# A cached-attention decode block with its gradients on one core: another order of the forward loop with three V loads ahead in place of five, zero-padded dO copies filled once by VectorE, and four copies of transposed V moved to VectorE

## Chip, cores and metric

The kernel runs on one core of one Trainium2 chip. The metric is device time in microseconds (us), the median of several executions.

## What is computed

The reference is one pre-layernorm decode block (batch 4, one new token, width 512) and the gradients of all its inputs but one:

```python
def _A_ref(x, k_cache, v_cache, wq, wo):          # B=4, H=32 heads, Dh=128, Sk=4096 cached rows
    q = (x @ wq).reshape(B, Sq, H, Dh).transpose(0, 2, 1, 3)
    scores = einsum("bhqd,bhkd->bhqk", q, k_cache) * (Dh ** -0.5)
    p = softmax(scores)
    o = einsum("bhqk,bhkd->bhqd", p, v_cache)
    return o.transpose(0, 2, 1, 3).reshape(B, Sq, H * Dh) @ wo
...
h  = x + _A_ref(layernorm(x), k_cache, v_cache, wq, wo)
h2 = h + (silu(layernorm(h) @ w1) * (layernorm(h) @ w3)) @ w2
out, vjp = jax.vjp(f, x, k_cache, v_cache, wq, wo, w1, w3, w2);  grads = vjp(grad_out)
```

There are 4 x 32 = 128 pairs of batch and head, called heads here. Each has a K and a V of 4096 x 128 bf16, which is 1 MB each. The forward part reads all K and V once (268 MB). The backward part reads all V again (134 MB) and writes the gradients of K and V (268 MB).

## The kernel before

The order of the instructions is written out by hand: every engine runs its instructions in the order of the program, and waits only where data or a buffer is not ready.

**Slots.** On-chip memory has 23 slots of about 1 MB (`NSLOT`, class `Slot`, L108). A list `free` hands out the slot that was given back longest ago, in the order of the program. A transfer into a slot waits on SP's queue until the slot's last user is done, and all later transfers wait behind it. Loads of K (`load_K`, L139, issued at L142) and of V (`load_V`, L146, issued at L150) take one slot each; so do a head's transposed K (`KT`), its product P*K (`PK`, with a column pair holding P), and every group of 16 results `M` (eight such slots by the end of the forward part). `more_K(s)` (L153) loads K ahead until head s + 6, as long as more than one slot is free; V is loaded `VQ` = 5 heads ahead.

**Forward loop** (L625, 64 groups `gi` of two heads, a = 2 gi and a + 1). For a group:

- `S_head` (L339) makes the scores of the group's heads on TensorE from the transposed K; it gives the KT slots back.
- `T_pe` (L316) and `T_dve` (L325) transpose the K of the next group's two heads, na and nb: a quarter on TensorE with a copy on ScalarE (L322, L323), three quarters on VectorE (L328).
- The softmax: `sm_max` (VectorE, L361 mx, L363 mxm), `sm_max_T` (TensorE, x_ps L368), `sm_gmax` (VectorE, gm L373), `sm_bcast` (TensorE, b_ps L378), `sm_exp` (VectorE nm L383, ScalarE E L386), `sm_sum` (TensorE, l_ps L392), `sm_norm` (VectorE rl L397, ScalarE Pn L400), `sm_P` (TensorE pt_P L407, ScalarE P_all L411).
- `PK_pairs` (GpSimd, L417) takes a PK slot and writes P pairs into it; `PK_mul` (VectorE, L421) multiplies K by P and gives the K slot back.
- `M_mm` (TensorE, L436) multiplies PK by V; `M_end` adds sums for dq (L446), copies the result (ScalarE, L452) and gives the PK and V slots back.

Before, group gi multiplies P*K for head a - 2 between mxm and gm, and for head a - 1 at its end; `M_mm` runs for heads a - 3 and a - 2. Every 32 heads, `kP_copy` and, later in the group, `kP_columns` move a sum out. After the loop a tail finishes heads 125 to 127 and multiplies by wo; in the last groups `weights` (L595) loads wo, w1 and w3 as slots come free.

**Middle.** One chain of small operations: layernorm, w1 and w3 products (gu_ps L848), their gradients, dO for the first 32 of the 128 heads (`dO_columns`, L743), first gradients of V (`grad_V`, L788, VectorE L781, written out from L792). V is loaded for the second time at L808 into whatever slots are free.

**Backward loop.** `front(s)` (L1177) transposes V of head s in four groups (`V_T`, L768: TensorE L775, ScalarE copy L776) and multiplies it with dO, using four zero-padded copies `zd` of a dO column (L1193). The copies are zeroed and filled by GpSimd (L1154, L1158). `more_V` makes gradients of V, `grad_K` those of K (VectorE L781), and each 1 MB result is written out on SP's queue.

Of the kernel before, what the change touches and what calls it, by code (L numbers as in the profile page):

```python
# [10 lines left out]
BF16 = mybir.dt.bfloat16  # L11
# [2 lines left out]
AX = mybir.AxisListType  # L14

G = 2
VQ = 5
SLOT = 4160
NSLOT = 23
JQ = 8  # L20
# [4 lines left out]
def kernel(  # L25
# [22 lines left out]
    nc = tc.nc  # L48
    P = nc.NUM_PARTITIONS
# [101 lines left out]


    def more_K(s):  # L153
        while len(Ks) + kdone["n"] < min(NH, s + 7) and len(free) > 1:
            load_K(len(Ks) + kdone["n"])

    kdone = {"n": 0}
# [133 lines left out]
    def M_of(s):  # L291
        return Ms[s // MC].f(MC * (Dh + 1)).rearrange("p (n c) -> p n c", c=Dh + 1)[:, s % MC, :]
# [77 lines left out]
    def sm_gmax(gi):  # L370
        st = hold[gi]
        st["gm"] = fw.tile([G, 1], FP32, tag="gm", name="gm")
        nc.vector.tensor_reduce(out=st["gm"][:], in_=st["x"][0:G, 0:P], axis=AX.X, op=ALU.max)  # L373
# [45 lines left out]
    def PK_mul(s):  # L419
        PK = PKs[s].t[:].rearrange("p (j c) -> p j c", c=PKW)  # L420
        nc.vector.tensor_tensor(  # L421
            out=PK[:, :, 0:Dh].rearrange("p j (r t) -> p j r t", t=2),
            in0=Ks[s].heads().rearrange("p j (r t) -> p j r t", t=2),
            in1=PK[:, :, None, Dh:PKW].to_broadcast([P, SJ, Dh // 2, 2]),
            op=ALU.mult,
        )
        Ks.pop(s).give()
        kdone["n"] += 1
# [9 lines left out]
    def M_end(s):  # L438
        w = s % 32
        PK = PKs[s].t[:].rearrange("p (j c) -> p j c", c=PKW)  # L440
        if w == 0:
            hold["kP"] = psK.tile([P, 4, Dh], FP32, name="kP_ps", tag="kP")
        for c in range(2):
            for q in range(4):
                j0 = (c * 4 + q) * 4
                nc.tensor.matmul(hold["kP"][32 * q:32 * (q + 1), :, :], lhsT=ones_window(w), rhs=PK[:, j0:j0 + 4, 0:Dh],  # L446
                                 start=(w == 0 and c == 0), stop=(w == 31 and c == 1), tile_position=(0, 32 * q))
        PKs.pop(s).give()
        Vs.pop(s).give()
        if s % MC == 0:  # L450
            Ms.append(Slot("M"))
        nc.scalar.copy(out=M_of(s), in_=hold["M"][:, 0:Dh + 1])  # L452

    def kP_copy():
        hold["ks"] = Slot("kP_sb")
        kP_sb = hold["ks"].f(4 * Dh).rearrange("p (c d) -> p c d", c=4)
        nc.scalar.copy(out=kP_sb, in_=hold["kP"][:])

    def kP_columns(s):
        ks = hold.pop("ks")  # L460
        kP_sb = ks.f(4 * Dh).rearrange("p (c d) -> p c d", c=4)
        kt_ps = psM.tile([P, PKW], FP32, tag="M", name="kt_ps")
        for c in range(4):
            nc.tensor.matmul(kt_ps[:, 0:H], lhsT=kP_sb[:, c, :], rhs=sel_f[:], start=(c == 0), stop=(c == 3))
        nc.scalar.copy(out=kPT[:, s - 31:s + 1], in_=kt_ps[:, 0:H])
        ks.give()

    def O_cols(s0, s1):
        nc.vector.tensor_copy(out=OT_f[:, s0:s1], in_=Ms[s0 // MC].f(MC * (Dh + 1)).rearrange("p (n c) -> p n c", c=Dh + 1)[
            :, s0 % MC:s0 % MC + s1 - s0, Dh])  # L470
        nc.vector.tensor_copy(out=OT_bf[:, s0:s1], in_=OT_f[:, s0:s1])
# [123 lines left out]
    def weights(gi):  # L595
        if gi in reserve:
            while nvl["n"] < NH and len(free) > reserve[gi]:
                load_V(nvl["n"])
            pump(reserve[gi])
# [14 lines left out]

    def O_cols_of(m):
        if m % MC == MC - 1 and m < NH - 1:
            O_cols(m - MC + 1, m + 1)

    def PK(s):
        PK_mul(s)
        more_K(s + 1)

    for gi in range(NGI):  # L625
        nxt = gi < NGI - 1
        a, na, nb = gi * G, gi * G + 2, gi * G + 3
        m1, m2 = a - 3, a - 2
        has1, has2 = m1 >= 0, m2 >= 0
        S_head(gi, 0)  # L630
        S_head(gi, 1)
        weights(gi)
        if nxt:
            q_stationaries(gi + 1)
            T_pe(na)
        sm_max(gi)
        if has2:
            PK(m2)
        if has1:
            M_mm(m1, 0, 16)  # L640
        if nxt:
            T_pe(nb)
        sm_max_T(gi)
        sm_gmax(gi)
        if nxt:
            T_dve(na, 1)
        if has1:
            M_mm(m1, 16, SJ)
            M_end(m1)
            load_V(m1 + VQ)  # L650
            if m1 % 32 == 31:
                kP_copy()
        sm_bcast(gi)
        weights(gi)
        sm_exp(gi)
        if nxt:
            T_dve(na, 2)
            T_dve(na, 3)
        if has2:
            PK_pairs(a - 1)  # L660
            M_mm(m2, 0, 16)
        sm_sum(gi)
        sm_norm(gi)
        if gi == NGI - 1:

            nc.scalar.sqrt(warm[:], warm[:])
        if has1:
            O_cols_of(m1)
        if nxt:
            T_dve(nb, 1)  # L670
            T_dve(nb, 2, 2)
        if has2:
            M_mm(m2, 16, SJ)
            M_end(m2)
            load_V(m2 + VQ)
            PK(a - 1)
        weights(gi)
        if has1 and m1 % 32 == 31:
            kP_columns(m1)
        sm_P(gi)  # L680
        PK_pairs(a)
        weights(gi)
        hold.pop(gi - 3, None)
        if 2 <= gi:
            step("d")

    PK(NH - 2)
    c1b.close()
    c1b = ExitStack()
    psT = c1b.enter_context(tc.tile_pool(name="psTm", bufs=4, space=bass.MemoryType.PSUM))  # L690
# [21 lines left out]
    O_cols(NH - MC, NH)  # L712
    attn_page(2)
    attn_page(3)
    kP_copy()
    kP_columns(NH - 1)
    weights(NGI)
    assert not pending
    c1b.close()
# [16 lines left out]
    dqT_bf = pers2.tile([P, NH], BF16, name="dqT_bf")  # L736
    dqr_bf = pers2.tile([NH, Dh], BF16, name="dqr_bf")

    dhT = pers2.tile([P, DC, B], BF16, name="dhT")
    dhT_f = pers2.tile([P, DC, B], FP32, name="dhT_f")  # L740


    def dO_columns(h0, h1, ps, tag):  # L743
        s0, s1 = h0 * B, h1 * B
        dOT_ps = ps.tile([P, 512], FP32, tag=tag, name="dOT_ps")
        for h in range(h0, h1):
            for jj in range(DC):
                nc.tensor.matmul(dOT_ps[:, h * B:(h + 1) * B], lhsT=wo_page(h)[:, h % 8, jj, :], rhs=dhT[:, jj, :],
                                 start=(jj == 0), stop=(jj == DC - 1))
        nc.vector.tensor_copy(out=dOT_bf[:, s0:s1], in_=dOT_ps[:, s0:s1])  # L750
        nc.vector.tensor_tensor(out=dOT_f[:, s0:s1], in0=dOT_bf[:, s0:s1], in1=OT_f[:, s0:s1], op=ALU.mult)

    def dO_rows(h0, h1, ps_, tag_):
# [14 lines left out]
    def V_T(s, ps, part=range(SJ // GW)):  # L768
        if s not in VTs:
            VTs[s] = V2s.pop(s)  # L770
        v = VTs[s].heads()
        for g in part:
            pt = ps.tile([P, GW, P], BF16, tag="tps", name="pt_tps")
            for i in range(GW):
                nc.tensor.transpose(pt[:, i, :], v[:, g * GW + i, :], ident_b[:])  # L775
            nc.scalar.copy(out=v[:, g * GW:(g + 1) * GW, :], in_=pt[:])  # L776

    P2s, first_gv = {}, []

# [158 lines left out]
    with ExitStack() as c2:  # L938
# [210 lines left out]

        rows = {}  # L1150
        dS2s = {}
        zd = [bw3.tile([P, 132], BF16, name=f"zd{i}", tag=f"zd{i}", bufs=1) for i in range(B)]
        for i in range(B):
            nc.gpsimd.memset(zd[i][:], 0.0)  # L1154

        def dO_window(s):
            if s < NH:
                nc.gpsimd.tensor_copy(out=zd[s % B][:, 32:132:67], in_=dOT_bf[:, s:s + 1].to_broadcast([P, 2]))  # L1158

        def P_pairs(s):  # L1160
            if s < NH and s not in P2s:
# [15 lines left out]
        def front(s):  # L1177
            hl = s % B
            if s not in VTs:
                for g in range(SJ // GW):  # L1180
                    V_T(s, psT, range(g, g + 1))
                    if hl == 0 and g == 0:
                        rows_out()
                    if hl == 0 and g == 2:
                        rows_T()
            VT = VTs[s].heads()
            if hl == 0:
                rows["acc"] = psD.tile([P, 512], FP32, tag="dP", name="dP_ps")
            dO_window(s + 2)
            for u in range(2):  # L1190
                for c in range(4):
                    j0 = 8 * c + 4 * u
                    nc.tensor.matmul(rows["acc"][32 * c:32 * (c + 1), :], lhsT=zq_window(zd[hl], 2 * hl + u),  # L1193
                                     rhs=VT[:, j0:j0 + 4, :], start=(hl == 0 and u == 0),
                                     stop=(hl == B - 1 and u == 1), tile_position=(0, 32 * c))
            if hl == B - 1:
                rows["ps"] = rows.pop("acc")
            sl = VTs.pop(s)
            (vring if len(V2s) + len(VTs) + len(vring) < NV2 else free).append(sl.i)
# [46 lines left out]
            if s < NH and s not in V2s and s not in VTs:  # L1246
                load_V2(nc.sync)

        for s in range(2):
            dO_window(s)  # L1250
        for s in range(3, 6):
            P_pairs(s)
        for s in range(L):
# [60 lines left out]
```

## Time and profile before

| | us |
|---|---|
| median of 3 runs | 1728.51 |
| lowest and highest run | 1726.37, 1729.18 |
| the profiled execution's own time | 1729.18 |
| span of that execution's profile | 1727.3 |
| busy: TensorE matmul, VectorE, ScalarE, GpSimd | 1266.5, 1222.4, 974.2, 495.6 |
| bytes moved by DMA | 707.51 MB, mean 410 GB/s |

The profile's page divides the span in 40 slices of 43 us. The forward loop's first scores start at 19.8 us; the scores of group 57 start at 595.36, those of the last group, 63, at 678.60 us. The first gradient of V starts on its way out at 726.72 us. The last compute instruction ends at 1691 us, and what follows is the end of the writes. In views by stretch, the last three columns are the granted TensorE clock, the busy share of the DMA engines and GB/s. "L322 <- DMA Kn" in a view of waits means that the engine stood at line 322 until a load of K had landed.

### The profile page before, as it was taken

The page shows a single profiled execution, that of the slowest core. Times are in us where ns is not written, and L with a number is a line of the kernel's source. Part 1 is how long each engine was busy: PE and PEld are TensorE (multiplying, and loading weights), DVE is VectorE, ACT ScalarE, POOL GpSimd, SP SyncE. Part 2 cuts the span into 40 slices and gives each one's busy share as a digit, 9 for nine tenths or more (in the row PEclk, how much of TensorE's full clock was granted, in tenths as well). Part 3 has the DMA queues.
Part 4 walks back from the last instruction along what each step waited for, and adds up shares of the span by engine and source line. Part 5 has one row for each costly group of instructions (what it writes and reads, how often), then busy time and mean ns, then how long its engine had stood idle before and what let it go on. Part 6 is the DMA issues. An engine that isn't in the chain of part 4 may idle for free.

```text
span 1727.3 us, 38444 instructions
## 1 busy us (share of the span) xinstructions
PE 1266.5 (73%) x16180; PEld 916.7 (53%) x16180; DVE 1222.4 (71%) x1294; ACT 974.2 (56%) x1502; POOL 495.6 (29%) x678
## 2 busy tenths in 40 slices
PE   5899888888888877877777664666767567676550
PEld 4677666666666655745555443544444334443330
DVE  5899889898899866577776655674557556665672
ACT  3465545454454433577766664776767566576540
POOL 1344444444443322143243120131102222220020
PEclk9999999999999988799988997986888777788785
DMA  9999999999999978899999999999999999999996
GB/s 402 425 424 424 423 423 425 424 419 417 421 419 407 424 311 296 358 404 425 425 425 426 425 425 426 425 425 426 423 421 421 418 419 415 420 417 418 416 418 279
DMA packets 101742, 707.51 MB, mean 410 GB/s; under 512 B 11052, under 2 KB 15288, under 8 KB 17600
## 3 DMA queue, kind: packets, MB, share of 16 engines
q1 hardware_dynamic: 101152, 704.95, 98.1%
q8 instruction: 127, 2.08, 0.5%
q14 instruction: 47, 0.39, 0.1%
q0 software_dynamic: 416, 0.10, 0.0%
HBM read 422.59 MB, written 282.34 MB: 408 GB/s over the span
## 4 chain that ended last, share of the span: by engine, by line
DMA 50%; ACT 2%; PE 1%; DVE 1%; issue 0%; DVEq 0%; SPq 0%; ACTq 0%; POOL 0%
DMA out_dram<-gv 20%; DMA out_dram<-gk 14%; DMA V<-in_A_v_cache_dram 13%; ACT V L776 1%; DMA out_dram<-gwo 1%; DMA out_dram<-gw 1%; DMA wq<-in_A_wq_dram 1%; PE pt_tps L775 1%; DVE gv L781 1%; DVE gk L781 1%; PE dP_ps L1193 0%; PE gps L957 0%; ACT dPr L1168 0%; DVEq L1309 0%; PE rep_ps L1144 0%
## 5 line engine op out<-in xcount | busy, mean ns | idle before, releaser
L776 ACT COPY V<-pt_tps 128x1024 bf16<-128x1024 bf16 x512 | 489.9, 1024 | 134.2 <-PE pt_tps L775 126.3
L775 PE MATMUL pt_tps<-ident_b,V 128*128 128x128 bf16 x4096 | 350.2, 245 | 195.0 <-ACT V L776 154.4
L775 PEld LDWEIGHTS <-V 128*128 128x128 bf16 x4096 | 299.5, 112 | 267.0 <-issue 201.7
L781 DVE TENSOR_TENSOR gv<-P,reps 128x4096 bf16<-128x4096 bf16 x125 | 286.3, 2293 | 194.3 <-DMA out_dram<-gv 96.0
L781 DVE TENSOR_TENSOR gk<-dS,reps 128x4096 bf16<-128x4096 bf16 x128 | 293.2, 2293 | 104.4 <-DMA out_dram<-gv 88.9
L436 PE MATMUL M_ps<-PK,Vn 128*128 128x130 bf16 x4096 | 287.7, 223 | 9.2 <-DVE PK L421 7.1
L421 DVE TENSOR_TENSOR PK<-Kn,PK 128x4096 bf16<-128x4096 bf16 x128 | 290.0, 2265 | 2.3 <-POOL PK L417 2.1
L436 PEld LDWEIGHTS <-Vn 128*128 128x128 bf16 x4096 | 259.1, 100 | 18.2 <-issue 10.9
L328 DVE STREAM_TRANSPOSE KT<-Kn 128x512 f32<-128x512 f32 (+1 forms) x321 | 244.0, 791 | 0.2 <-issue 0.2
L323 ACT COPY KT<-pt_tps 128x1024 bf16<-128x1024 bf16 x128 | 129.4, 1012 | 194.2 <-PE pt_tps L322 163.2
L1193 PE MATMUL dP_ps<-V,zd 128*32 128x512 bf16 x1024 | 179.6, 430 | 68.8 <-ACT V L776 66.1
L1163 POOL COPY P<-P_all 128x64 bf16<-128x64 bf16 x125 | 94.6, 758 | 446.1 <-DVE gv L781 446.0
L417 POOL COPY PK<-P_all 128x64 bf16<-128x64 bf16 x128 | 74.0, 578 | 402.2 <-ACT P_all L411 267.7
L1158 POOL COPY zd<-dOT_bf 128x2 bf16<-128x2 bf16 x128 | 126.5, 989 | 168.8 <-PE dP_ps L1193 168.6
L334 POOL TENSOR_TENSOR W<-qrep,wmask 128x128 bf16<-128x128 bf16 x128 | 153.3, 1197 | 19.7 <-DVE qrep L286 14.5
L322 PE MATMUL pt_tps<-ident_b,Kn 128*128 128x128 bf16 x1024 | 83.5, 228 | 80.0 <-DMA Kn<-in_A_k_cache_dram 79.8
L1193 PEld LDWEIGHTS <-zd 128*32 128x32 bf16 x1024 | 37.4, 95 | 156.6 <-issue 141.9
L322 PEld LDWEIGHTS <-Kn 128*128 128x128 bf16 x1024 | 61.4, 102 | 108.3 <-DMA Kn<-in_A_k_cache_dram 104.0
L400 ACT ACTIVATE Pn<-E,rl 128x1024 bf16<-128x1024 f32 x64 | 73.7, 1151 | 49.5 <-DVE rl L397 44.4
L446 PE MATMUL kP_ps<-PK,onesw 128*32 128x512 bf16 x1024 | 81.1, 394 | 0.0
L354 PE MATMUL S_ps<-KT,W 128*32 128x256 bf16 x1536 | 75.0, 286 | 0.5 <-DVE KT L328 0.2
L411 ACT COPY P_all<-pt_P 32x64 bf16<-32x64 bf16 x256 | 52.1, 204 | 38.0 <-PE pt_P L407 35.7
(239 smaller groups left out, 1206.8 us busy)
## 6 DMA issues: line engine op xcount, KB each, us to landing
Kn<-in_A_k_cache_dram SPq DMA_DIRECT2D x128, 1024.0 KB, 14.1
Vn<-in_A_v_cache_dram SPq DMA_DIRECT2D x128, 1024.0 KB, 13.4
V<-in_A_v_cache_dram SPq DMA_DIRECT2D x128, 1024.0 KB, 20.0
out_dram<-gv SPq DMA_DIRECT2D x128, 1024.0 KB, 20.0
out_dram<-gk SPq DMA_DIRECT2D x128, 1024.0 KB, 20.1
wq<-in_A_wq_dram SPq DMA_DIRECT2D x8, 1024.0 KB, 15.4
out_dram<-gw SPq DMA_DIRECT2D x6, 896.0 KB, 19.9
wo<-in_A_wo_dram SPq DMA_DIRECT2D x4, 1024.0 KB, 8.1
```

The lines of the kernel that those rows point to most:

```text
L322: nc.tensor.transpose(pt[:, i, :], Kn[:, c * GW + i, :], ident_b[:])
L323: nc.scalar.copy(out=KT[:, c * GW:(c + 1) * GW, :], in_=pt[:])
L328: nc.vector.transpose(out=KT[:, c * w_:(c + n) * w_], in_=Kn[:, c * w_:(c + n) * w_])
L334: nc.gpsimd.tensor_tensor(out=W[:, hl], in0=qrep[:, :, s:s + 1].to_broadcast([P, 4, 32]), in1=wmask[:, hl, None, :].to_broadcast([P, 4, 32 ...
L421: nc.vector.tensor_tensor(out=PK[:, :, 0:Dh].rearrange("p j (r t) -> p j r t", t=2), in0=Ks[s].heads().rearrange("p j (r t) -> p j r t", t=2),
L436: nc.tensor.matmul(hold["M"][:], lhsT=Vn[:, j, :], rhs=PK[:, j, :], start=(j == 0), stop=(j == SJ - 1))
L775: nc.tensor.transpose(pt[:, i, :], v[:, g * GW + i, :], ident_b[:])
L776: nc.scalar.copy(out=v[:, g * GW:(g + 1) * GW, :], in_=pt[:])
L781: nc.vector.tensor_tensor(out=dst.rearrange("p j (r t) -> p j r t", t=2), in0=col2[:, :, None, :].to_broadcast([P, SJ, Dh // 2, 2]), in1=r ...
L1158: nc.gpsimd.tensor_copy(out=zd[s % B][:, 32:132:67], in_=dOT_bf[:, s:s + 1].to_broadcast([P, 2]))
L1163: nc.gpsimd.tensor_copy(out=P2s[s][:], in_=P_all[:, s, :, None].to_broadcast([P, SJ, 2]))
L1193: nc.tensor.matmul(rows["acc"][32 * c:32 * (c + 1), :], lhsT=zq_window(zd[hl], 2 * hl + u), rhs=VT[:, j0:j0 + 4, :], start=(hl == 0 and u ...
```

## The change

In the forward loop the order within a group is another one: `M_mm` for head a - 3 now comes right behind the scores; `T_dve(na, 1)`, not a P*K product, stands between mxm and gm; both P*K products of a group, for heads a - 1 and a, stand in its second half, the second as its last VectorE instruction. `VQ` is 3 in place of 5, and K is loaded up to one head further (`s + 8`). `kP_copy` and `kP_columns` become one `kP_flush` right behind `M_end`. In the middle, `zd` is one tile that GpSimd zeroes early, and one VectorE instruction fills it for the first four heads; for heads 1 to 4, VectorE copies the second of the four groups of transposed V.

```diff
-VQ = 5
+VQ = 3
...
-        while len(Ks) + kdone["n"] < min(NH, s + 7) and len(free) > 1:
+        while len(Ks) + kdone["n"] < min(NH, s + 8) and len(free) > 1:
...
     for gi in range(NGI):
...
         S_head(gi, 1)
         weights(gi)
+        if has1:
+            M_mm(m1, 0, 16)
+        sm_max(gi)
         if nxt:
             q_stationaries(gi + 1)
             T_pe(na)
-        sm_max(gi)
-        if has2:
-            PK(m2)
-        if has1:
-            M_mm(m1, 0, 16)
-        if nxt:
-            T_pe(nb)
+            T_dve(na, 1)
         sm_max_T(gi)
-        sm_gmax(gi)
-        if nxt:
-            T_dve(na, 1)
         if has1:
             M_mm(m1, 16, SJ)
+        sm_gmax(gi)
+        sm_bcast(gi)
+        if nxt:
+            T_dve(na, 2)
+        sm_exp(gi)
+        if has1:
             M_end(m1)
             load_V(m1 + VQ)
...
-        sm_bcast(gi)
-        weights(gi)
-        sm_exp(gi)
+        if hasp:
+            PK_pairs(pk1)
         if nxt:
-            T_dve(na, 2)
             T_dve(na, 3)
-        if has2:
-            PK_pairs(a - 1)
-            M_mm(m2, 0, 16)
+            T_pe(nb)
+            T_dve(nb, 1)
         sm_sum(gi)
         sm_norm(gi)
...
-        if nxt:
-            T_dve(nb, 1)
-            T_dve(nb, 2, 2)
+        if hasp:
+            PK_mul(pk1)
+            more_K(pk1 + 1)
+        weights(gi)
         if has2:
-            M_mm(m2, 16, SJ)
+            M_mm(m2, 0, 24)
+        sm_P(gi)
+        if has2:
+            M_mm(m2, 24, SJ)
             M_end(m2)
             load_V(m2 + VQ)
-            PK(a - 1)
         weights(gi)
-        sm_P(gi)
         PK_pairs(a)
+        if nxt:
+            T_dve(nb, 2, 2)
+        PK_mul(a)
+        more_K(a + 1)
         weights(gi)
...
+    zd = pers2.tile([P, B, 132], BF16, name="zd")
+    nc.gpsimd.memset(zd[:], 0.0)
...
         nc.vector.tensor_copy(out=dOT_bf[:, s0:s1], in_=dOT_ps[:, s0:s1])
+        if s0 == 0:
+            nc.vector.tensor_copy(out=zd[:, :, 32:132:67], in_=dOT_bf[:, 0:B, None].to_broadcast([P, B, 2]))
...
-            nc.scalar.copy(out=v[:, g * GW:(g + 1) * GW, :], in_=pt[:])
+            if 0 < s < 5 and g == 1:
+                nc.vector.tensor_copy(out=v[:, g * GW:(g + 1) * GW, :], in_=pt[:])
+            else:
+                nc.scalar.copy(out=v[:, g * GW:(g + 1) * GW, :], in_=pt[:])
...
-        zd = [bw3.tile([P, 132], BF16, name=f"zd{i}", tag=f"zd{i}", bufs=1) for i in range(B)]
-        for i in range(B):
-            nc.gpsimd.memset(zd[i][:], 0.0)
...
-            if s < NH:
-                nc.gpsimd.tensor_copy(out=zd[s % B][:, 32:132:67], in_=dOT_bf[:, s:s + 1].to_broadcast([P, 2]))
+            if B <= s < NH:
+                nc.gpsimd.tensor_copy(out=zd[:, s % B, 32:132:67], in_=dOT_bf[:, s:s + 1].to_broadcast([P, 2]))
...
-        for s in range(2):
-            dO_window(s)
```

In the diff, `m1` is a - 3, `m2` is a - 2 and `pk1` is a - 1; `has1`, `has2`, `hasp` and `nxt` only guard the first and last groups.

More of the change, by code (lines that the diff above doesn't have):

```diff
@@ L447, in M_end @@
                                  start=(w == 0 and c == 0), stop=(w == 31 and c == 1), tile_position=(0, 32 * q))
-        PKs.pop(s).give()
-        Vs.pop(s).give()
         if s % MC == 0:
@@ L452, in M_end, with kP_flush @@
         nc.scalar.copy(out=M_of(s), in_=hold["M"][:, 0:Dh + 1])
-    def kP_copy():
-        hold["ks"] = Slot("kP_sb")
-        kP_sb = hold["ks"].f(4 * Dh).rearrange("p (c d) -> p c d", c=4)
+        PKs.pop(s).give()
+        Vs.pop(s).give()
+    def kP_flush(s):
+        ks = Slot("kP_sb")
+        kP_sb = ks.f(4 * Dh).rearrange("p (c d) -> p c d", c=4)
         nc.scalar.copy(out=kP_sb, in_=hold["kP"][:])
-    def kP_columns(s):
-        ks = hold.pop("ks")
-        kP_sb = ks.f(4 * Dh).rearrange("p (c d) -> p c d", c=4)
         kt_ps = psM.tile([P, PKW], FP32, tag="M", name="kt_ps")
@@ L613 @@
             T_dve(s, c)
[L617 to L623, printed above, removed]
     for gi in range(NGI):
@@ L628 @@
         m1, m2 = a - 3, a - 2
-        has1, has2 = m1 >= 0, m2 >= 0
+        pk1 = a - 1
+        has1, has2, hasp = 0 <= m1 < NH, 0 <= m2 < NH, 0 <= pk1 < NH
         S_head(gi, 0)
@@ L651 @@
             if m1 % 32 == 31:
-                kP_copy()
-        sm_bcast(gi)
-        weights(gi)
-        sm_exp(gi)
+                kP_flush(m1)
+            if m1 % MC == MC - 1 and m1 < NH - 1:
+                O_cols(m1 - MC + 1, m1 + 1)
+        if hasp:
+            PK_pairs(pk1)
         if nxt:
-            T_dve(na, 2)
             T_dve(na, 3)
-        if has2:
-            PK_pairs(a - 1)
-            M_mm(m2, 0, 16)
+            T_pe(nb)
+            T_dve(nb, 1)
         sm_sum(gi)
@@ L666 @@
             nc.scalar.sqrt(warm[:], warm[:])
-        if has1:
-            O_cols_of(m1)
-        if nxt:
-            T_dve(nb, 1)
-            T_dve(nb, 2, 2)
+        if hasp:
+            PK_mul(pk1)
+            more_K(pk1 + 1)
+        weights(gi)
         if has2:
-            M_mm(m2, 16, SJ)
+            M_mm(m2, 0, 24)
+        sm_P(gi)
+        if has2:
+            M_mm(m2, 24, SJ)
             M_end(m2)
             load_V(m2 + VQ)
-            PK(a - 1)
         weights(gi)
-        if has1 and m1 % 32 == 31:
-            kP_columns(m1)
-        sm_P(gi)
         PK_pairs(a)
+        if nxt:
+            T_dve(nb, 2, 2)
+        PK_mul(a)
+        more_K(a + 1)
         weights(gi)
@@ L685 @@
             step("d")
-    PK(NH - 2)
     c1b.close()
@@ L714 @@
     attn_page(3)
-    kP_copy()
-    kP_columns(NH - 1)
+    kP_flush(NH - 1)
     weights(NGI)
@@ L1192, in front @@
                     j0 = 8 * c + 4 * u
-                    nc.tensor.matmul(rows["acc"][32 * c:32 * (c + 1), :], lhsT=zq_window(zd[hl], 2 * hl + u),
+                    nc.tensor.matmul(rows["acc"][32 * c:32 * (c + 1), :], lhsT=zq_window(zd[:, hl], 2 * hl + u),
                                      rhs=VT[:, j0:j0 + 4, :], start=(hl == 0 and u == 0),
```

## The prediction

> **What bounds the kernel now.** I read the page's slices first, then waits by stretch, then the DMA by ten-us stretches, then SP's own timeline.
>
> ```profile
> DMA  9999999999999978899999999999999999999996
> GB/s 402 425 424 424 423 423 425 424 419 417 421 419 407 424 311 296 358 404 425 425 425 426 425 425 426 425 425 426 423 421 421 418 419 415 420 417 418 416 418 279
> ```
>
> The DMA is full nearly everywhere, at some 424 GB/s, so one 1.0486 MB load costs 2.47 us and a group's four loads 9.88. An instruction saved on an engine is worth nothing there. But slices 15 to 17 (605 to 735 us) fall to 296 to 358.
>
> Waits of TensorE, from 100 to 600 us and then from 606 to 680 us (total, times, longest):
>
> ```profile
> PE pt_tps L322 <- DMA Kn<-in_A_k_cache_dram: 53.2, 87, 1.7
> ```
>
> ```profile
> PE pt_tps L322 <- DMA Kn<-in_A_k_cache_dram: 20.1, 7, 5.9
> ```
>
> In the steady loop K comes a little late at each transpose: the loop is DMA-bound. In the last groups the same wait is up to 5.9 us, yet the DMA is idle beside it:
>
> ```profile
> 600.00:610.00 10.00, 8.61 (x141) 6.79 (x141) 7.94 (x15) 5.09 (x11) 2.12 (x7) 1.00 1.01 426
> 610.00:620.00 10.00, 8.77 (x143) 6.81 (x141) 9.75 (x13) 4.88 (x11) 4.00 (x6) 1.00 0.97 370
> 620.00:630.00 10.00, 4.64 (x38) 3.53 (x39) 2.14 (x5) 1.28 (x2) 2.24 (x5) 0.66 0.58 241
> ...
> 640.00:650.00 10.00, 9.06 (x126) 7.12 (x127) 6.42 (x10) 4.48 (x11) 0.24 (x1) 0.83 0.62 227
> ```
>
> ```profile
> 629.36 3.69 SPq L150 DMA_DIRECT2D Vn<-in_A_v_cache_dram  x2
> 633.10 1.85 SPq L142 DMA_DIRECT2D Kn<-in_A_k_cache_dram  x2
> 644.19 3.42 SPq L150 DMA_DIRECT2D Vn<-in_A_v_cache_dram  x2
> 647.66 1.65 SPq L142 DMA_DIRECT2D Kn<-in_A_k_cache_dram  x2
> ```
>
> SP issues a group's four loads in one burst, waits ten us, then the next burst. I followed the list of free slots through the program: in group 57 the eighth M slot is taken, and 8 M + 5 V + 2 KT + 2 PK leave 6 of 23 for K. From then on, V of heads a + 2 and a + 3 waits for the slot that this group's own `M_end` gives back, and both K behind it on SP's queue are wanted one group later. So loads and compute take turns: the scores of group 57 start at 595.36, those of 63 at 678.60, six groups in 83.2 us, 13.9 each where the loads need 9.88. From 610 to 760 us the 15 stretches have a mean of 329.9 GB/s: 150 x (1 - 329.9 / 425) = **33.6 us of DMA time lost**, 29.2 of it before the first gradient leaves at 726.72. That is also the most that this change can win.
>
> **The change, part by part.** The sum is made against the profiled execution's own 1729.2 us; the median is 0.7 lower.
>
> *Slots.* The same list followed through the changed order: at eight M slots, K keeps 7 and V 3. In group 58 the four loads wait for, in order, the scores (V116), `M_end` of head 113 (K122), `PK_mul` of 115 (V117), `M_end` of 114 (K123): spread over the group, and wanted 14, 17, 12 and 15 us later by the clock below. Landing takes 14.1 us for K and 13.4 for V now (page, part 6), which is 5 to 6 loads in flight; 12 us of lead leave room for about 4 ahead of it, so the DMA stays full. The burst goes. What is late next is V at `M_mm`, in place of K at `T_pe`, and behind it in TensorE's order the whole softmax; but it is late only while the DMA is full.
>
> *The loop without waits for data.* VectorE, starting at its last product (t = 0): product 2.17 to the start of mx (405.37 to 407.54), mx and mxm to 2.75, a transpose 0.62 (pitch) to 3.4, gm 0.2, a transpose to 4.2. TensorE meanwhile: scores 0.2 to 1.25, `M_mm` 16 x 0.065 = 1.04 to 2.3, `T_pe` 0.55, x_ps 0.2, `M_mm` 1.04 to 4.14, then b_ps; nm follows 0.48 after b_ps starts (411.54 to 412.02), at 4.62: VectorE idle 0.4. Two transposes to 5.95. On TensorE b_ps 0.3, `M_end` 0.55, `T_pe` 0.55, l_ps at 5.55; rl 0.42 later at 5.97. Product to 8.3, double transpose 1.2 to 9.5. ScalarE: E 0.6, M copy 0.25, KT copy (1.01) to 6.6, Pn 1.15 to 7.75, pt_P 0.65, P_all 0.85 to 9.3, pairs and the last product 0.35 later: **9.65 us a group**. With 7 or more M slots (groups 49 to 62) the last pairs wait for the PK slot of the same group's `M_end`, at 9.65: some 9.95. Before, an unhindered group takes 9.07 (scores at 52.34 and 61.41), so this order is 0.6 to 0.9 slower by itself, and 9.88 of DMA hides the first of it, barely.
>
> *Pairs on GpSimd* take 0.24 us beside transposes and 1.10 when VectorE is in a product (401.15 and 406.62); I take 0.24, since they fall beside the double transpose; the other end costs up to 0.9 a group. [...]
>
> *kP_flush* in place of a copy and later matmuls: TensorE stands for the copy (0.59) and runs kt_ps (1.08) ahead of l_ps, 2 to 2.5 us in 3 groups. Loads in flight cover it; bare, it is 7 us.
>
> *Where group 63 comes to stand.* Groups 0 and 1 lack work to hide latency, as now; group 2 starts at some 44 us (now 42.82, plus the product in front of mx). At 9.65, group 57 could start at 44 + 55 x 9.65 = 575; the DMA keeps it back. In its order of loads V113 is the 239.75th MB-sized load (with 5.75 for wq and w2), 251.4 MB, and by 600 us 251.9 MB had moved: so group 58 can't run before 598.5, group 57 not before 588.6. I take 590, and 6 x 9.95 to group 63: **650, against 678.6: 28.6 us**. If the early groups are as now, it is 655 and 23.5.
>
> *Tail.* In group 63 no product stands between mxm and gm any more (681.04 to 683.38): 2.2 us off the chain that leads to the middle. Together 30.8, beyond what the DMA can give back by then (29.2). Its work to the end of the w loads is 256.2 MB by 610 plus 18.3 plus 7.9 MB: 671.7 us; the w products are wanted 24.3 after group 63's scores, 674; seven V loads follow to 689, and the first gradient leaves 45.9 after the scores, at 696. So it stays nearly full. I take **27.5**: 29.2 less some 1.7 for joints.
>
> *Middle.* GpSimd's zeroing (0.65) and first fills go; dP_ps waited 2.53 us for them, until 730.07. It then waits for ScalarE's V copy, which ends at 728.47: 1.5 us earlier, for one VectorE cast of 0.18 in front of dOT_f. *V copies*: four of ScalarE's 0.94 go, four of VectorE's 0.69 (the same shape at L220) come, in its queue behind gradients of 2.29. For heads 1 and 2 TensorE waits longer for a buffer (up to 1.4 us each); for 3 and 4, where VectorE is idle 3.5 us (before 750.68), 0.9 each is won. Bounds: 3 won to 3 lost, as the DMA is full again from 757 us. I take 0 for both.
>
> Sum: 1729.2 - 27.5 = 1701.7, so a median of **1702**.
>
> [...] After its waits of 3.3 to 5.9 us TensorE's eight transposes take 1.03 to 1.04 us, not 0.62, and 16 `M_mm` 1.94, not 1.10: about 1.7 us a group. [...] By the rows, waits of up to 1.7 us (100 to 600) left the granted clock at 1.00; I count nothing.
>
> **Rivals.**
> - *Forecast (0.60)*: 1695 to 1708.
> - *The new loop is itself the bound (0.20).* If a group takes 10.2 in place of 9.65, group 63 starts at 44 + 61 x 10.2 = 666: 12.6 + 2.2 won, 1714; at 10.4, 1726. For it: margins of 0.25 us, ScalarE's KT copy just ahead of Pn. Against: none of the terms is larger than its row. Range 1708 to 1725.
> - *Slower (0.13): three V are too few.* V117's lead of 12.3 us is below the 13.4 that V takes now, and its wait stands in front of transposes, softmax and product. If a group then pays the missing 1.1 us without the DMA being full, it takes 10.8: group 63 at 44 + 61 x 10.8 = 703, 24 - 2 lost, 1751. It decides from (680.8 - 44) / 61 = 10.44 us a group on. Against: a late load is a busy DMA, and fewer loads in flight land sooner.
> - *It does not reach the end of the forward part (0.04)*: if the bursts have another cause than slots, K remains late and only the tail's 2.2 us go, 1727.
> - *More (0.03)*: all 33.6 us, 1695, and less if the backward start gains too.
>
> **Numbers.** A difference of 0.2% (3.5 us) is about what can be told from none. Faster by more: 0.60 + 0.20 + 0.03 = 0.83; within it 0.04; slower 0.13. For 8 in 10 the range goes from 1693 (all of the loss, and 2 of the 3 us at the start of the backward part) to 1722, which leaves out the slower case and the worst of the second.
>
> **What would show it.** Right: GB/s above 415 from 610 to 690; SP's four issues spread over the group; group 63's scores at 645 to 658; waits at L436 for V of around 1 us in place of those at L322. Wrong: DMA share below 1 between 100 and 600, or groups more than 10 us apart with the DMA idle (second case), or with waits for V above 3 us and a granted clock below 1 (third); K waits of 5 us from 610 on (fourth). From 760 on nothing should differ but the start.

## The result and the profile after

| | before | after |
|---|---|---|
| median (lowest to highest), us | 1727.91 (1726.37 to 1729.18, 4 runs) | 1703.05 (1702.31 to 1703.57, 4 runs) |
| ratio, 95% interval | | 0.9856 [0.9839, 0.9873] |
| profiled execution's own time | 1729.18 | 1703.14 |
| its span | 1727.3 | 1701.2 |
| bytes moved, mean GB/s | 707.51 MB, 410 | 707.50 MB, 416 |

The changed kernel is 24.9 us faster; the forecast was 1702. The same bytes move at a higher mean rate. Where the rate rose is read from the slices of the changed kernel's page (43 us each):

```profile
DMA  9999999999999999999999999999999999999996
GB/s 401 424 425 423 424 424 425 423 423 422 416 424 413 423 405 398 394 394 426 425 425 426 425 425 426 425 426 426 425 420 421 420 423 417 418 421 417 415 416 283
```

The hole of slices 15 to 17 (311, 296, 358 before) is now 405, 398, 394. Slice 18 is 394 for 404, and the other slices hardly differ. Ten-us stretches of the changed kernel (busy us and instructions of TensorE, weight loads, VectorE, ScalarE, GpSimd; then granted clock, DMA share, GB/s):

```profile
610.00:620.00 10.00, 8.30 (x146) 6.82 (x142) 9.25 (x13) 4.87 (x12) 2.92 (x6) 1.00 0.96 375
620.00:630.00 10.00, 8.32 (x145) 6.84 (x142) 9.24 (x13) 4.87 (x12) 2.90 (x6) 1.00 1.00 421
...
640.00:650.00 10.00, 8.29 (x145) 6.81 (x141) 9.24 (x13) 4.87 (x12) 2.92 (x6) 1.00 1.02 419
```

Every stretch from 610 to 650 us now holds one whole group: the same 145 matmuls, VectorE 9.24 us busy, and a granted clock of 1.00, where before a stretch was alternately full (VectorE 9.75) and empty (2.14, clock 0.66). SP's own queue in the changed kernel:

```profile
623.24 0.33 SPq L150 DMA_DIRECT2D Vn<-in_A_v_cache_dram  x1
623.94 0.33 SPq L142 DMA_DIRECT2D Kn<-in_A_k_cache_dram  x1
625.04 0.33 SPq L150 DMA_DIRECT2D Vn<-in_A_v_cache_dram  x1
629.24 0.33 SPq L142 DMA_DIRECT2D Kn<-in_A_k_cache_dram  x1
633.25 0.33 SPq L150 DMA_DIRECT2D Vn<-in_A_v_cache_dram  x1
```

The four loads of a group go out one at a time, 10.01 us apart from group to group (623.24 and 633.25). The waits of TensorE from 606 to 680 us in the changed kernel:

```profile
PE x_ps L368 <- DVE mxm L363: 6.6, 6, 1.4
```

The wait for K at L322 (20.1 us, longest 5.9) is gone altogether; what is left is the softmax's own chain: 1.1 us a group at x_ps, and at pt_P (L407) 3.0 us in five waits. From 100 to 600 us the waits have moved from K to V, and from the transposes to `M_mm`:

```profile
PE M_ps L436 <- DMA Vn<-in_A_v_cache_dram: 26.8, 40, 1.2
PE x_ps L368 <- DVE mxm L363: 24.0, 32, 1.1
```

One yardstick serves for all runs below: the DMA time lost between 600 and 750 us, 150 x (1 - mean GB/s of its 15 stretches / 425). Before it is 33.2 us, after 10.7; the difference, 22.5, carries most of the span's 26.1.

### The profile page after: what moved, and what is told of

It is laid out like the page before. It is cut to its first block, busy times and chain, and to the rows that moved or that the text cites. A ratio compares the mean times of both kernels' runs of the same rounds, so it can differ in the third digit from the quotient of the medians.

```text
span 1701.2 us, 38402 instructions
## 1 busy us (share of the span) xinstructions
PE 1238.0 (73%) x16180; PEld 913.4 (54%) x16180; DVE 1238.9 (73%) x1299; ACT 964.8 (57%) x1498; POOL 397.8 (23%) x671
## 2 busy tenths in 40 slices
DMA packets 101741, 707.50 MB, mean 416 GB/s; under 512 B 11052, under 2 KB 15288, under 8 KB 17600
## 3 DMA queue, kind: packets, MB, share of 16 engines
q8 instruction: 127, 2.08, 0.5%
## 5 line engine op out<-in xcount | busy, mean ns | idle before, releaser
L421 DVE TENSOR_TENSOR PK<-Kn,PK 128x4096 bf16<-128x4096 bf16 x128 | 292.4, 2284 | 26.1 <-POOL PK L417 25.7
L436 PE MATMUL M_ps<-PK,Vn 128*128 128x130 bf16 x4096 | 285.8, 222 | 30.7 <-DMA Vn<-in_A_v_cache_dram 29.8
L436 PEld LDWEIGHTS <-Vn 128*128 128x128 bf16 x4096 | 253.1, 99 | 50.9 <-DMA Vn<-in_A_v_cache_dram 43.4
L328 DVE STREAM_TRANSPOSE KT<-Kn 128x512 f32<-128x512 f32 (+1 forms) x321 | 250.7, 797 | 0.3 <-issue 0.2
L1155 POOL COPY P<-P_all 128x64 bf16<-128x64 bf16 x125 | 98.6, 790 | 449.3 <-DVE gv L777 432.9
L334 POOL TENSOR_TENSOR W<-qrep,wmask 128x128 bf16<-128x128 bf16 x128 | 123.0, 961 | 83.1 <-PE S_ps L354 68.5
L417 POOL COPY PK<-P_all 128x64 bf16<-128x64 bf16 x128 | 32.6, 255 | 414.2 <-ACT P_all L411 411.2
L322 PE MATMUL pt_tps<-ident_b,Kn 128*128 128x128 bf16 x1024 | 80.5, 223 | 0.0
L446 PE MATMUL kP_ps<-PK,onesw 128*32 128x512 bf16 x1024 | 79.6, 388 | 0.0
L386 ACT ACTIVATE E<-S_ps,nm 128x256 f32<-128x256 f32 x64 | 30.4, 474 | 81.8 <-DVE nm L383 81.8
L322 PEld LDWEIGHTS <-Kn 128*128 128x128 bf16 x1024 | 62.0, 100 | 25.9 <-issue 25.8
## 6 DMA issues: line engine op xcount, KB each, us to landing
out_dram<-gk SPq DMA_DIRECT2D x128, 1024.0 KB, 20.1
wo<-in_A_wo_dram SPq DMA_DIRECT2D x4, 1024.0 KB, 11.6
```

Of the source, the lines that this page charges most:

```text
L322: nc.tensor.transpose(pt[:, i, :], Kn[:, c * GW + i, :], ident_b[:])
L328: nc.vector.transpose(out=KT[:, c * w_:(c + n) * w_], in_=Kn[:, c * w_:(c + n) * w_])
L334: nc.gpsimd.tensor_tensor(out=W[:, hl], in0=qrep[:, :, s:s + 1].to_broadcast([P, 4, 32]), in1=wmask[:, hl, None, :].to_broadcast([P, 4, 32 ...
L421: nc.vector.tensor_tensor(out=PK[:, :, 0:Dh].rearrange("p j (r t) -> p j r t", t=2), in0=Ks[s].heads().rearrange("p j (r t) -> p j r t", t=2),
L436: nc.tensor.matmul(hold["M"][:], lhsT=Vn[:, j, :], rhs=PK[:, j, :], start=(j == 0), stop=(j == SJ - 1))
L1155: nc.gpsimd.tensor_copy(out=P2s[s][:], in_=P_all[:, s, :, None].to_broadcast([P, SJ, 2]))
```

## The experiments

All were timed against the kernel before on their own chip. The first eight ran on one chip, in two groups with the kernel before at 1726.73 (1725.71 to 1728.14, 7 runs) and 1726.50 (1725.66 to 1727.79, 7 runs); the last three on another, with 1726.57 (1725.82 to 1728.19, 7 runs). "Start of group 63" is the start of its mx (L361).

| run | median (range) us | ratio [95%] | span | start of group 63 | DMA lost, 600 to 750 |
|---|---|---|---|---|---|
| before | 1727.91 | 1 | 1727.3 | 680.60 | 33.2 |
| changed | 1703.05 (1702.31 to 1703.57) | 0.9856 [0.9839, 0.9873] | 1701.2 | 657.11 | 10.7 |
| 1 old order, V 3, K + 1 | 1700.73 (1700.55 to 1702.27) | 0.9851 [0.9837, 0.9866] | 1698.7 | 654.22 | 7.0 |
| 2 new order, V 5 | 1715.28 (1714.72 to 1715.87) | 0.9934 [0.9919, 0.9949] | 1712.9 | 669.63 | 19.5 |
| 3 changed, no V copies on VectorE | 1701.72 (1701.20 to 1701.91) | 0.9854 [0.9838, 0.9871] | 1699.9 | 658.0 | 8.5 |
| 4 changed, forward part alone | 1703.47 (1701.57 to 1704.81) | 0.9865 [0.9850, 0.9879] | 1701.0 | 657.4 | 9.6 |
| 5 changed, old zd | 1706.47 (1705.20 to 1709.94) | 0.9887 [0.9873, 0.9902] | 1703.3 | 657.2 | 11.5 |
| 6 run 1 and the new zd | 1701.16 (1700.82 to 1702.07) | 0.9854 [0.9839, 0.9869] | 1699.0 | 653.9 | 6.6 |
| 7 old order, V 4 | 1702.68 (1701.51 to 1703.05) | 0.9863 [0.9846, 0.9879] | 1699.7 | 655.20 | 8.1 |
| 8 changed, K one less ahead | 1703.74 (1703.43 to 1705.33) | 0.9870 [0.9855, 0.9885] | 1701.7 | 654.00 | 9.8 |
| 9 changed again | 1703.59 (1702.85 to 1705.03) | 0.9866 [0.9852, 0.9881] | 1700.9 | 657.1 | 9.3 |
| 10 run 1 again | 1700.99 (1700.78 to 1701.50) | 0.9851 [0.9836, 0.9865] | 1698.9 | 653.7 | 7.2 |
| 11 run 3 again | 1701.49 (1700.76 to 1702.04) | 0.9854 [0.9838, 0.9871] | 1698.7 | 657.2 | 8.0 |

The column on the right explains most of the span: span less DMA lost lies between 1690.5 and 1694.1, and between 1690.5 and 1692.4 in all but the kernel before and run 2. So these kernels differ mainly by how far the DMA stays below its full rate in this stretch; a difference of under 2 us between two of them can't be read from this column alone.

### Which half of the change wins: slots or order

**Run 1**, the slots alone in the old order:

```diff
-VQ = 5
+VQ = 3
...
-        while len(Ks) + kdone["n"] < min(NH, s + 7) and len(free) > 1:
+        while len(Ks) + kdone["n"] < min(NH, s + 8) and len(free) > 1:
```

> The kernel before, in its own order, with only the loads' lead of the change: V 3 heads ahead and K up to s + 8. Theory 'slots' (the time came from K running out of slots in the last six groups): its free list now keeps 8 K, the groups from 58 on stand about 9.9 us apart in place of 14 to 17, GB/s from 610 to 680 us is above 400, and the median is 1698 to 1706. Rival 'order' (the time came from the new order of the loop, which gives K slots back sooner): the bursts stay, groups of 14 us or more, median 1722 to 1730.

Measured: 1700.73, 26.0 us below its before. The starts of groups 57 to 63 stand 11.82, 9.22, 9.73, 9.88, 9.94 and 8.92 us apart, where they took 13.9 on average. Its stretches and its SP queue:

```profile
610.00:620.00 10.00, 8.91 (x143) 6.90 (x142) 9.83 (x15) 5.56 (x14) 3.78 (x8) 1.00 1.02 424
620.00:630.00 10.00, 8.47 (x141) 6.80 (x141) 9.32 (x14) 5.19 (x14) 3.57 (x6) 1.00 1.01 423
...
640.00:650.00 10.00, 9.57 (x159) 7.91 (x160) 9.12 (x13) 4.98 (x11) 4.50 (x6) 1.00 1.01 423
```

```profile
619.07 4.24 SPq L150 DMA_DIRECT2D Vn<-in_A_v_cache_dram  x2
623.40 1.64 SPq L142 DMA_DIRECT2D Kn<-in_A_k_cache_dram  x2
```

Two lines of the program give the whole gain. And SP still issues two V and two K close together, as it did before; yet the DMA stays at 423 GB/s. So the burst by itself does not starve TensorE. What starved it was how short before its use a K load left the queue. Before, K of head 125 leaves SP's queue at 647.66; TensorE is ready for it at 651.04, 3.4 us later, and stands 5.51 us until it has landed:

```profile
656.55 1.04 PE L322 MATMUL pt_tps<-ident_b,Kn 128*128 128x128 bf16 x8 [5.51 <-DMA Kn<-in_A_k_cache_dram]
```

Call the time from leaving the queue to the moment when TensorE is ready for these transposes the lead of the load. Here it is for heads 120 to 127, and beside it the median time from issue to landing of the K loads from 606 to 660 us:

| kernel | lead of K, us | landing, us | wait at L322, 606 to 680 us |
|---|---|---|---|
| before | 9.6, 3.4, 16.9, 3.4, 14.4, 3.4, 16.4, 3.3 | 9.2 | 20.1 |
| run 1 | 11.6 to 21.4 | 11.5 | none |
| changed | 16.1 to 22.9 | 10.8 | none |
| run 2, below | 6.1 to 10.6 | 8.2 | 8.1 |
| run 7, below | 10.4 to 11.9 | 11.4 | 2.6 |

Before, every second K load has a lead of 3.3 or 3.4 us, far below its landing, and there TensorE stands; with the slots of the change the shortest is 11.6 in run 1 and 16.1 in the changed kernel, and that wait is gone.

**Run 2**, the order alone (the changed kernel with the old slots):

```diff
-VQ = 3
+VQ = 5
...
-        while len(Ks) + kdone["n"] < min(NH, s + 8) and len(free) > 1:
+        while len(Ks) + kdone["n"] < min(NH, s + 7) and len(free) > 1:
```

> The changed kernel with only the loads' lead of the kernel before: V 5 heads ahead, K up to s + 7. Theory 'slots': with eight M slots the list leaves 5 or 6 for K, K of the next group is issued half a group ahead of its use, the last groups stand 14 us or more apart with waits for K at L322, and the median is 1720 to 1735. Rival 'order': groups stay at 10.0 us, 1701 to 1706.

Measured: 1715.28, and that is a miss: the order by itself wins 11.4 us. Its waits of TensorE from 606 to 680 us, and one of its emptiest stretches:

```profile
PE pt_tps L322 <- DMA Kn<-in_A_k_cache_dram: 8.1, 5, 2.8
PE x_ps L368 <- DVE mxm L363: 5.4, 5, 1.4
```

```profile
650.00:660.00 10.00, 8.85 (x135) 7.48 (x133) 8.53 (x11) 4.47 (x9) 2.90 (x6) 0.88 0.83 297
```

K is still late, but by 8.1 us in place of 20.1, and the last six groups take 9.99 to 13.57 (669.63 - 609.86 = 59.8 for five of them, and 10.56 for the first). Its SP queue issues the loads singly, as the changed kernel's does:

```profile
639.54 0.33 SPq L150 DMA_DIRECT2D Vn<-in_A_v_cache_dram  x1
640.26 0.33 SPq L142 DMA_DIRECT2D Kn<-in_A_k_cache_dram  x1
643.52 0.33 SPq L150 DMA_DIRECT2D Vn<-in_A_v_cache_dram  x1
```

The shortest lead is 6.1 us, between the 3.4 of before and the landing. So with few slots for K, the new order, which gives slots back at four places of the group, recovers part of the loss. Which of the moved steps does it was not taken apart; among them is `M_end`, which now gives its slots back behind its copy of M and not ahead of it. The two halves don't add: 26.0 and 11.4 alone, 24.9 together. Both shorten the same wait for K.

**Run 7**, one slot in the old order:

```diff
-VQ = 5
+VQ = 4
```

> The kernel before with V 4 heads ahead in place of 5, nothing else: the list leaves 7 slots for K at the end in place of 6. Theory 'slots, by the lead of the last K': one slot more puts the second K of a group one group ahead of its use, and the bursts vanish altogether: groups from 58 on 9.9 us apart, 1699 to 1704. Rival 'each slot is worth its share': half the gain, 1711 to 1717.

Measured: 1702.68. The dose is not graded: seven slots for K remove nearly all of the starvation (groups 58 to 63 are 9.22, 9.22, 9.33, 9.94, 9.79 us apart behind one of 12.89; the wait for K from 606 to 680 us falls from 20.1 us to the line below), and an eighth adds 2 us at most, which these runs can't tell from nothing (medians 1700.73 and 1702.68, ranges that overlap).

```profile
PE pt_tps L322 <- DMA Kn<-in_A_k_cache_dram: 2.6, 5, 0.7
620.00:630.00 10.00, 9.24 (x147) 7.08 (x143) 9.80 (x14) 5.54 (x12) 4.17 (x9) 1.00 1.01 424
```

This also speaks against reading run 1 as an effect of the shorter V lead: here V keeps four heads.

### Is the new loop itself a bound

**Run 8**, the changed kernel with K one head less ahead:

```diff
-        while len(Ks) + kdone["n"] < min(NH, s + 8) and len(free) > 1:
+        while len(Ks) + kdone["n"] < min(NH, s + 7) and len(free) > 1:
```

> The changed kernel with K only up to s + 7. The free list then gives the last pairs of groups 49 to 56 a slot that a product gave back, not the same group's M_end: groups of 9.74 to 9.85 us there in place of 10.00; from group 58 on nothing changes (7 K either way) and they stay at 10.00. Worth 1 to 2 us at group 63, median 1701 to 1703. If the 10.00 has another cause than the PK slot, it stays in 49 to 56, and the median stays at 1703 or rises by the K lost.

In the changed kernel, groups 50 to 62 take 10.00 us (group 57 takes 10.55), more than the 9.88 of their loads. GpSimd and VectorE at the end of group 60:

```profile
634.60 0.25 POOL L417 COPY PK<-P_all 128x64 bf16<-128x64 bf16 x1 [6.36 <-ACT P_all L411]
```

```profile
633.14 1.24 DVE L328 STREAM_TRANSPOSE KT<-Kn 128x1024 f32<-128x1024 f32 x1
634.89 2.29 DVE L421 TENSOR_TENSOR PK<-Kn,PK 128x4096 bf16<-128x4096 bf16 x1 [0.51 <-POOL PK L417]
```

VectorE stands 0.51 us for the pairs, and these wait for a PK slot that the same group's `M_end` gives back at about 634.5. (The view names P_all, which ended at 634.33; `M_end`'s last read of the slot, L446, ended at 634.46.) With one K less the free list hands `PK_pairs` an older slot: in run 8 groups 50 to 56 take 9.74 (583.54 to 593.27, for one), where the pairs start at 581.05, before that L446 ends at 581.12; from group 58 on it is 10.00 again, and group 63 starts at 654.00, 3.1 earlier. The cause of the 10.00 is shown. But the time doesn't follow, and that part of the expectation is a miss: 1703.74. Its later stretches:

```profile
650.00:660.00 10.00, 7.92 (x136) 6.37 (x134) 6.72 (x9) 3.67 (x10) 2.04 (x2) 1.00 0.95 364
660.00:670.00 10.00, 10.00 (x152) 7.38 (x150) 5.50 (x4) 3.29 (x10) 0.95 (x3) 1.00 1.02 331
```

What run 8 wins from 600 to 620 us (422 and 415 GB/s for 400 and 375) it gives back from 650 to 670 (364 and 331 for 394 and 359): by 690 us its DMA has lost 4.3 us and that of the changed kernel 4.7. So the loop's own pace is no term of the sum while the DMA is full, and the place of group 63 is not the time either; the rate at which bytes go is.

### zd and the V copies

**Run 3**, the V copies alone undone:

```diff
-            if 0 < s < 5 and g == 1:
-                nc.vector.tensor_copy(out=v[:, g * GW:(g + 1) * GW, :], in_=pt[:])
-            else:
-                nc.scalar.copy(out=v[:, g * GW:(g + 1) * GW, :], in_=pt[:])
+            nc.scalar.copy(out=v[:, g * GW:(g + 1) * GW, :], in_=pt[:])
```

> The changed kernel with all four copies of transposed V on ScalarE for every head, as before; the filled zd stays. By the prediction (both ends of 3 us, 0 taken): 1703, within 1. Rival 'the copies cost': dP of heads 2 to 4 ends 4 us later after the first gradient than it would, in a stretch where the DMA is not full, so that without them the median is 1699 to 1701.

Measured: 1701.72, between the two. **Run 5**, zd alone undone, so that GpSimd zeroes and fills all copies again:

```diff
-    zd = pers2.tile([P, B, 132], BF16, name="zd")
-    nc.gpsimd.memset(zd[:], 0.0)
...
-        if s0 == 0:
-            nc.vector.tensor_copy(out=zd[:, :, 32:132:67], in_=dOT_bf[:, 0:B, None].to_broadcast([P, B, 2]))
...
+        zd = [bw3.tile([P, 132], BF16, name=f"zd{i}", tag=f"zd{i}", bufs=1) for i in range(B)]
+        for i in range(B):
+            nc.gpsimd.memset(zd[i][:], 0.0)
...
-            if B <= s < NH:
-                nc.gpsimd.tensor_copy(out=zd[:, s % B, 32:132:67], in_=dOT_bf[:, s:s + 1].to_broadcast([P, 2]))
+            if s < NH:
+                nc.gpsimd.tensor_copy(out=zd[s % B][:, 32:132:67], in_=dOT_bf[:, s:s + 1].to_broadcast([P, 2]))
```

> The changed kernel with zd zeroed and filled by GpSimd as before, and VectorE's four copies of transposed V kept; it is to be compared with the forward loop alone (1703.5) and with the kernel without the copies (1701.7). Theory 'the copies cost because they stand behind gradients in VectorE's queue': dP of heads 1 to 3 ends 2 to 4 us later after the first gradient, median 1704 to 1707. By the prediction, which took 0: 1703.5, within 1.

Measured: 1706.47. **Run 4**, the edits of runs 3 and 5 together, which leaves the changed forward part with the old middle and backward part:

> The forward loop of the change with the whole backward part of before: zd zeroed and filled by GpSimd, all V copies on ScalarE. By the prediction (0 for both edits of the backward part): 1703, within 1. Rival 'zd is worth 2, the copies cost 4': 1701 to 1702, and 2 above the kernel that only drops the copies.

Measured: 1703.47. These three stood on one chip. Run 5 less run 4 prices the copies without the new zd: 3.0 us lost. Run 4 less run 3 prices the new zd: 1.7 won, with ranges that overlap. The wait that goes with zd is in run 4's trace, and in run 3's it is not:

```profile
704.85 1.04 PE L1182 MATMUL dP_ps<-V,zd 128*32 128x512 bf16 x8 [2.53 <-POOL zd L1147]
```

**Run 6** puts the new zd on run 1:

```diff
+    zd = pers2.tile([P, B, 132], BF16, name="zd")
+    nc.gpsimd.memset(zd[:], 0.0)
...
+        if s0 == 0:
+            nc.vector.tensor_copy(out=zd[:, :, 32:132:67], in_=dOT_bf[:, 0:B, None].to_broadcast([P, B, 2]))
```

> The order of the kernel before with V 3 heads and K 8 ahead, plus the zd filled by VectorE, without VectorE's V copies. If slots and zd are what counts, the two add up: 1700.7 less 1.5 to 2, so 1698 to 1700, below the changed kernel. If the new order of the loop had a part of the gain of its own, it is above 1701.

Measured: 1701.16 against 1700.73 of run 1. A miss: head 0 is earlier (its dP starts 3.2 us behind the first gradient, 5.7 in run 1), and nothing comes of it. So zd is worth between nothing and 1.7 us. Run 3 less run 6 also prices the new order once the slots are there: 0.6 us lost, and run 4 less run 1, both with the old zd, 2.7 lost. The ranges overlap in both pairs; in neither does the order win anything.

### The three versions on one chip

**Run 9** is the changed kernel, **run 10** is run 1, **run 11** is run 3.

> The changed kernel itself once more, on the same chip as the two runs that follow. So far 1703.05 (1702.31 to 1703.57) against 1701.72 without VectorE's V copies and 1700.73 for the old order with the changed slots, but those stood on other chips. Theory (the parts of the change differ, if little): 1703 +- 1 here, with the other two below it. Rival (differences between chips): all three within 1.0 us of each other.

> The kernel before with three V ahead and one more K, nothing else (the same edit as in the first run of this study). Theory: 1700.2 to 1701.5, so 1.5 to 3 us faster than the changed kernel on the same chip: the slots are the whole gain, and the new order, zd and V copies together cost a little. Rival: within 1.0 us of the changed kernel, the old lead being one between chips.

> The changed kernel with ScalarE making all copies of V. Theory: 1701.2 to 1702.2, some 1.3 us faster than the changed kernel on the same chip, because VectorE's copies stand behind its products while TensorE waits for them. Rival: within 0.5 us of the changed kernel, the copies costing nothing once the DMA is full again.

Measured: 1703.59, 1700.99 and 1701.49, the first with a range that touches neither of the others. The slots alone are 2.6 us faster than the whole change; V copies on VectorE cost 2.1 of it. What a copy does, in run 9, on VectorE and then on TensorE:

```profile
706.40 2.29 DVE L777 TENSOR_TENSOR gv<-P,reps 128x4096 bf16<-128x4096 bf16 x1 [0.81 <-DMA out_dram<-gv]
708.61 0.68 DVE L770 COPY V<-pt_tps 128x1024 bf16<-128x1024 bf16 x1
709.21 4.48 DVE L777 TENSOR_TENSOR gv<-P,reps 128x4096 bf16<-128x4096 bf16 x2
```

```profile
706.90 0.61 PE L768 MATMUL pt_tps<-ident_b,V 128*128 128x128 bf16 x8 [1.10 <-ACT V L772]
707.44 0.39 PE L1185 MATMUL dP_ps<-V,zd 128*32 128x512 bf16 x1
709.34 1.04 PE L1185 MATMUL dP_ps<-V,zd 128*32 128x512 bf16 x7 [1.52 <-DVE V L770]
710.32 1.89 PE L768 MATMUL pt_tps<-ident_b,V 128*128 128x128 bf16 x16
```

In run 11 the same head 1:

```profile
706.56 0.76 PE L1182 MATMUL dP_ps<-V,zd 128*32 128x512 bf16 x3
707.85 0.59 PE L1182 MATMUL dP_ps<-V,zd 128*32 128x512 bf16 x5 [0.54 <-ACT V L769]
```

The copy of 0.68 us stands behind a gradient of 2.29 on VectorE, so TensorE's dP waits 1.52 for it, and the work after that wait runs slower: seven matmuls in 1.04 and sixteen transposes in 1.89, where 16 take 1.05 at 703.44. The stretch of 710 to 720 us, in run 9 and then in run 11:

```profile
710.00:720.00 10.00, 7.59 (x68) 5.40 (x66) 7.17 (x6) 4.63 (x5) 3.09 (x6) 0.67 0.99 397
```

```profile
710.00:720.00 10.00, 7.31 (x84) 4.54 (x84) 9.72 (x5) 7.72 (x10) 8.75 (x6) 1.00 1.02 405
```

TensorE is busy for about as long (7.59 and 7.31) but gets 68 matmuls done instead of 84, at a granted clock of 0.67 instead of 1.00. Head 4's last five dP matmuls start at 727.54 in run 9 and at 723.74 in run 11: 3.8 us later, of which 2.1 reach the end.

## Why the prediction was right, step by step

**What bounds the kernel: right.** The loop was DMA-bound, the last groups starved for slots, and the lost DMA time was the most that could be won. Run 1 and run 7 show the slots as the cause. One reading was loose: that "SP issues a group's four loads in one burst" is not by itself what starves TensorE, since runs 1 and 7 keep the burst and lose less DMA time (7.0 and 8.1 us) than the changed kernel (10.7).

**The size: right, in part by luck.** Taken was 27.5 us; the span fell by 26.1. Before the backward part nearly all is won: the first gradient starts at 698.37 in place of 724.40, 26.0 earlier. But 28.6 us for the scores of group 63 was too much: they start 24.3 earlier (654.30 in place of 678.60). The step that failed is "I take 590" for the start of group 57: 588.6 was the bound that the bytes set, and the group's scores came at 593.73, against 595.36 before. The branch "if the early groups are as now, it is 655 and 23.5" was the one that came. The change exchanges what is loaded ahead rather than adding to it: for heads 112 to 115 the lead of K is 20.8 to 22.4 us in place of 11.1 to 12.0, and that of V at `M_mm` 10.7 to 16.2 in place of 21.0 to 23.5; that this is why group 57 is hardly earlier is argued, not tested. The forecast didn't rest on the 28.6, as it was held down to the lost DMA time of 29.2 less 1.7 "for joints", and run 8 bears that out: group 63 3.1 us earlier, and no time won. The joints came to 5.1 us (401 GB/s from 610 to 700.63 us). Gains that the sum doesn't have made up for a part: 1.6 us in the loop from 100 to 600 us (a mean of 420.8 GB/s before and 422.2 now). And the sum's 1701.7 is the profiled execution's time; less the 0.7 that the prediction itself names, its median is 1701.0, not 1702.

**The loop's pace: right within 0.1.** 9.74 us a group in the middle of the loop (9.65 worked out), 10.00 in groups 50 to 62 but one (9.95), and the named cause, the PK slot of the same group's `M_end`, is shown by run 8. `kP_flush` makes groups of 12.61, 12.38 and 11.96, so 2.2 to 2.9 above 9.74 (2 to 2.5 worked out). Pairs on GpSimd: 0.24 us median over 128, as taken. Not foreseen: groups that move a result of O run to 10.6, with VectorE waiting up to 0.85 for ScalarE's copy of M.

**The tail: right.** From mx of group 63 to the first gradient 41.26 us, 43.80 before: 2.5 for the 2.2 worked out.

**zd: right in place, little in time.** Against the first gradient, head 0's dP starts 2.5 us earlier and ends 1.7 earlier in run 3 than in run 4, for the 1.5 worked out. It was costed at nothing in the sum, since the DMA is full again behind it; the runs put it between 0 and 1.7.

**V copies: the mis-sized term.** Taken as 0 between 3 won and 3 lost; measured 2.1 lost (run 9 and run 11) to 3.0 lost (runs 5 and 4), the edge of the bounds. The delay for heads 1 and 2 came about as written: the longer waits add 1.8 us for head 1 (1.10 and 1.52 in run 9, 0.31 and 0.54 in run 11) and 1.0 for head 2 (1.10 and 0.77, 0.31 and 0.54). "For 3 and 4 [...] 0.9 each is won" did not: TensorE's clock fell after those waits (0.67 from 710 to 720 us in run 9, 1.00 in run 11), and heads 2 to 4 came 3.0 to 4.3 us later in run 9 than in run 11.

**The rivals.** The loop as a bound: refuted, groups of 10.00 left the DMA at 419 to 422 GB/s from 620 to 650 us and run 8's quicker loop gained nothing. Slower, three V too few: refuted; in the changed kernel V waits at L436 are at most 1.2 us from 100 to 600 us, at a granted clock of 0.98 to 1.00 in the five stretches of 100 us from 100 on. Does not reach the end: refuted by the first gradient. "GB/s above 415 from 610 to 690" came only in four of the eight stretches (375, 394, 359 and 415 in the others): the new kernel is not free of loss, and run 1 loses 3.7 us less.

## What to carry to other kernels

Where loads share a pool of buffers with results, follow the list of free buffers through the program and ask how far ahead of its use each load is issued; a pool that is one buffer short in the last tenth of a loop cost 24 us here, and a constant repaired it. When a change bundles a prefetch depth with a rewritten order, run the depth alone first: here it was the whole gain and 2.6 us more than the bundle. Copies moved to an engine that has idle time on average can still cost, if they stand behind that engine's long instructions while another engine waits (2.1 us here, run 9 against run 11).

## What the runs showed of the hardware beyond the expected

- In the changed kernel TensorE's clock was lower behind short waits. In run 9 no single wait of TensorE between 702 and 711 us is above 1.52 us, and in the changed kernel's profiled run none is above 2.06; yet the granted clock of 710 to 720 is 0.67 and 0.50, and sixteen transposes take 1.89 us rather than 1.05. TensorE was busy 5.69 of the 10 us before, in run 9; in run 11, with 6.79 busy and waits of at most 0.70 from 702 us on, the clock stayed at 1.00. What lowered it there was not tested. The prediction counted nothing for the clock, from waits of up to 1.7 us in the loop that left it at 1.00; in the changed kernel's loop it stayed at 0.98 to 1.00 from 100 to 600 us, and the place where it did fall was not looked at.
- Behind one wait of 2.08 us in a busy loop it was lower, too. In run 1 groups 21, 28, 36, 43 and 57 take 11.8 to 12.2 us; TensorE's longest wait for V from 100 to 600 us is 2.3, and the granted clock of that stretch is 0.98, where it is 1.00 in the kernel before. In group 57 TensorE stands 2.08 us for V, and the granted clock of 600 to 610 us is 0.83. In the kernel before, a wait of 2.12 us for K ends at 600.73, and the granted clock of 600 to 610 us is 1.00. TensorE in group 57 of run 1, where 16 `M_mm` take 1.10 at 606.68, in the group that follows:

```profile
600.36 1.52 PE L436 MATMUL M_ps<-PK,Vn 128*128 128x130 bf16 x16 [2.08 <-DMA Vn<-in_A_v_cache_dram]
602.07 1.89 PE L436 MATMUL M_ps<-PK,Vn 128*128 128x130 bf16 x16
```

  So with three V ahead the old order pays something for late V, while the changed order waits 1.2 us at most from 100 to 600 us. Why V is late in just these groups stays open.
- A full DMA is not always one at 424 GB/s. The DMA view of the changed kernel, from 640 to 650 us and then from 660 to 670:

```profile
DMA packets 574, 4.19 MB, mean 419 GB/s; under 512 B 64, under 2 KB 64, under 8 KB 64
```

```profile
DMA packets 3241, 3.59 MB, mean 359 GB/s; under 512 B 52, under 2 KB 3118, under 8 KB 3240
```

In the second the weights wo (L550, issued from 653.26 to 662.84 us) are landing, and behind them the first of w (L544): packets of some 1.1 KB (3.59 MB / 3241), a DMA share of 1.09 and 359 GB/s. In run 1 it is 390 there, at a share of 1.08; run 8's 331 is idle time in part. This part of the "lost" time is not idle time that another order of the loop could fill. Whether longer packets would win it back wasn't tried.
